# RWKV6 attention and an exact-GELU MLP in one kernel: the interleaving order of six of its eight stages rewritten

## The chip, the cores and the metric

The kernel runs on one core of a Trainium2 chip. A core has several engines that work side by side, each through its own queue in order: TensorE (PE in the profile, with its weight loads as a row of their own, PEld), VectorE (DVE), ScalarE (ACT), GpSimd (POOL) and SyncE (SP), which here only issues transfers. The metric is the time on the device in microseconds (us). Before the change the median of three runs is 587.15 us (586.81 to 588.11).

## The reference

Two blocks follow each other. The first is a recurrent attention over 4 batches, 8 heads, 768 tokens and 48 channels a head:

```python
for t in range(S):
    cur = np.einsum('bhd,bhe->bhde', u[None] * kt, vt)
    y[:, :, t] = np.einsum('bhd,bhde->bhe', rt, state + cur)
    state = wt[:, :, :, None] * state + np.einsum('bhd,bhe->bhde', kt, vt)
```

Its result, laid out as 3072 tokens by 384 channels, goes through an MLP with 2048 hidden channels:

```python
h = x @ w_in
g = 0.5 * h * (1.0 + erf(h * inv_sqrt2))
return g @ w_out
```

All data are float32.

## The kernel before, in words

**Passes and stages.** The 768 tokens of each batch are cut in two, so there are 8 pieces of 384 tokens. The outer loop (L1403) has a pass x for each, 0 to 7; "stage n" is the pass x = n. A stage runs the MLP of the piece before, `mlp(x-1)`, beside the attention of its own piece, `attention(x)`, and the beginning of the attention that follows, `attention(x+1)`. Behind stage 7, `mlp(7)` runs alone.

**Streams, pieces and the plan.** Each of these functions is a generator, and what it issues between two `yield`s is a piece. The order in which the engines get their instructions is written out by hand: `PLAN[x]` is a string, and each letter takes the next piece from one stream. `.` is `mlp(x-1)`; `s` the rest of `attention(x)`; `f` the beginning of `attention(x+1)`; `l` the loads of the next piece of r, w, k and v (`load`, L180); `x` the sums of this piece's MLP input that the next MLP wants (`sums_of_x`, L941; in stage 7 `sums_of_x15`, L984); `w` in stage 2 the sums of the weights (`first_sum`, `h_sums`, L895, L920) and in stage 7 those of `sums_of_w15` (L959); `c` converts weights in stages 0 and 1. A letter whose stream is at its end, or empty, does nothing. Behind the string the streams are emptied in the order `. s l x w`:

```python
        for c in PLAN[x]:
            next(streams[c], None)
        for c in ".slxw" if x == 0 else ".slxwc":
            while next(streams[c], streams) is not streams:
                pass
        slots = following
```

So a plan sets the order of the pieces in every engine's queue at once, and the order in which tiles are taken from the pools. Within a stream the order is fixed.

**The MLP** computes its products by schemes with fewer multiplications (7 block products where 8 would be needed), so that VectorE adds where TensorE would multiply.
- `h_halves` (L1028; MLPs 2 to 6) goes through four values of q. Each piece is one group of matmuls on 128x192 blocks (L1024), `first(q)` to `seventh(q)`; `first`, `fifth` and `sixth` are 2 matmuls, the others 4. `first` and `fifth` take a bank of the tag "mm", of which there are two; ScalarE copies results to the `u` banks or applies the Gelu (L1053, L1056, L1087, L1091), and `third` and `seventh` end in a VectorE addition (L1078, L1096). The order is first, third(q-1), seventh(q-1), second, fifth, sixth, fourth(q-1); `fourth(3)` is done late, inside the first product.
- The MLP of stage 2, `mlp(1)`, still goes through 16 whole h blocks (L1231 to L1246: 3 matmuls of 128x384 at L1236, then a Gelu at L1239).
- The second half is made of products (`product`, L1248): 8 matmuls at L1250, with a `yield` behind the fourth, so that a plan places half products. Each matmul has two records in the trace. Even MLPs have 7 products and 2 more that end in L1344 and L1347; odd MLPs have 7 and 5 more, and end in the addition L1373 after L1358, L1363, L1366 and L1369. `of_g` (L1010) makes the sums that the products need. The products also use the two "mm" banks, under the name `o_ps`.
- `h_fifteen` (L1140) is the form of `mlp(7)`.

**The attention** (`attention`, L366), from stage 2 on, is a chain of pieces:
1. VectorE multiplies out decays and products of r and k (L404 to L453; L404 is the first, and with L391 and `apart` it builds the sums within blocks of four tokens).
2. The layout for the first level: ScalarE's copies L573, VectorE's L578 and L579.
3. Bursts of 64x64 matmuls (L604), each into a pair of PSUM banks. There are two pairs from stage 2 on. The first level has three "fine" bursts of 20, 20 and 8 + 16 matmuls, the last with those of L595; the copies that empty them are VectorE's L637, and two "fine copies" at L687. At the second level odd pieces have three bursts of 20, 20 and 8 matmuls (the last 16 records in the trace, and it takes the pair of banks that the first leaves), even pieces one burst in three parts, the third part in the `u` banks. ScalarE's copies L620 empty these; a copy out of the `u` banks is twelve instructions, the others six.
4. Between them VectorE scales r and k (L658 to L669), and transposes blocks of k (L552); twelve moves of such blocks go through SyncE's queue (L547), eight from one piece and four from the next.
5. L749 multiplies the transposed k with v; it waits for those twelve moves. Then VectorE chains the states (L771, L773).
6. `inside()` (L802) multiplies within the chunks, into the pair `y_ps`; a ScalarE copy of the last result column, the *fence* (L815; in stage 0 VectorE's L812), stands behind it. The next piece (L845) adds the part of the states into the same banks; ScalarE copies the result to the MLP's input `xT` (L868), and through `ysb` (L871) and SyncE's transfers L875.

In each stage TensorE goes to and fro between the MLP's 128-wide matmuls and the attention's 64x64 ones; one stay with the second kind is called a visit below.

Of the kernel before, what the change touches and what calls it, by code (L numbers as in the profile page):

```python
# [41 lines left out]
        ".cswc.ccc.cccss.lc.ccscs..cc.cs.cclwcsc.ccssc.c.cccsccc..ssccc.c.lcls.cc.ccsc.w.clwscclccc"  # L42
        ".c.swcw.ss.ccs.lcsc..cwcccslccslff..w..fw.wfs..f..flffffffww"
    ),
    2: "...l...s..ws.swssswssss.sslsw...ssss.sssws.ll..ws.w..lw.sw.wl.sls.sls..lf.s....sf..f.f.xx.fxl.x.x",
    3: "l..sss..s.s..s.s....s...s.ssllss.sss.s.s.ss.l..lsss..sssss.sls.s..s......s..ls.llssf.sf.sflf.f.x.x..xxfffxf",
    4: "...s...lsl......s.s....sss..ssss..s..ss..s..s...llssslss....s.slss...s...sll.sl.s.sfs..fsf.ff..xl.x.xfffxffx",
    5: ".l..........ls.ss...s.sslls.ssss..ss.sls...sss..sssssl.ss.s..s.......s.lssll.sfsf.f.s.ff.x..x.xxxl",
    6: "sss.sls.....s......ls.s....s.sssssss..s.....s.ss....s.s.ssss.s.l.ss.l.ls.l...s.l.lslssf..s.ffs..lff.xx..xffxffx",
    7: "......s.s....s.s...s.ssssss...sss.ss...sss..ssss.s...ss.ww.ww.wwsw.ww.ww.ws.s.ss.s.ww.swww.swwwwwwww.wwww.www.xxxx.xxxxxx",  # L50
}


# [1436 lines left out]
```

## Time and profile before

| what | value |
| --- | --- |
| median of three runs | 587.15 us |
| the profiled execution's own time | 589.49 us |
| its span in the trace | 587.3 us |
| granted TensorE clock, mean | 0.997 |
| matmuls of the first half of the MLPs 2 to 6 with the two "mm" banks (L1024, `h_ps`) | 408, 81.4 us |
| matmuls of the h blocks (L1236) | 192, 64.1 us |
| first matmul of the MLP in stage 3, 4, 5, 6, 7 | 191.4, 255.7, 327.2, 391.4, 462.1 us |
| first matmul of `mlp(7)` | 526.8 us |
| HBM traffic, mean over the span | 70 GB/s |

The profile comes from one execution. Its lines give, for each engine, what ran when, and in brackets how long the engine had been idle before and what released it: `[0.31 <-PE d L604]` reads "idle for 0.31 us until TensorE's work at line 604 on the tile d was done". Start-to-start times of consecutive matmuls say what a matmul costs when TensorE is kept fed; the duration of one matmul record is longer, because matmuls overlap.

### The profile page before, as it was taken

To read this page: it belongs to the slowest core of one execution; us is meant where nothing else is said; L and a number is where in the kernel's file an instruction comes from. 1 tells how busy PE (TensorE), PEld (TensorE's weight loads), DVE (VectorE), ACT (ScalarE), POOL (GpSimd) and SP (SyncE) were. 2 spreads that over 40 slices of the span, in tenths; PEclk is the share of its full clock that TensorE was granted. 3 is DMA by queue.
4 is the path that set the end of the run, shared out by engine and by line. 5 is a ranking of instruction groups with operands and counts; after the bars stand their busy time and mean duration, and the time that the engine had idled before them with its cause. 6 is when DMAs were issued, how large, how long until landed. Compare 5 with 4: busy or idle time off the path is not lost. (4 is left out here: it accounts for less than half of the span.)

```text
span 587.3 us, 17363 instructions
## 1 busy us (share of the span) xinstructions
PE 572.2 (97%) x7505; PEld 508.6 (87%) x7517; DVE 460.5 (78%) x817; ACT 286.5 (49%) x668; POOL 8.0 (1%) x21
## 2 busy tenths in 40 slices
PE   7789999999999999999999999999999999999998
PEld 3576666766899999999999999999999999999997
DVE  6879766999969986787859987598768998975532
ACT  2468889322722558146462458245562465623400
POOL 3100000000000000000000000000000000000000
PEclk9989999999999999999999999999999999999999
DMA  7659661120142301341023310430015200210000
GB/s 241 207 159 356 217 213 56 36 87 2 31 139 79 110 2 32 97 126 38 1 39 106 124 39 18 97 104 19 2 28 168 73 3 1 41 40 8 1 15 33
DMA packets 51003, 46.79 MB, mean 80 GB/s; under 512 B 31728, under 2 KB 36080, under 8 KB 50928
## 3 DMA queue, kind: packets, MB, share of 16 engines
q1 hardware_dynamic: 50832, 45.62, 25.7%
q8 instruction: 59, 0.97, 0.7%
q14 instruction: 16, 0.13, 0.1%
q10 hardware_dynamic: 96, 0.07, 0.0%
HBM read 36.24 MB, written 4.72 MB: 70 GB/s over the span
## 5 line engine op out<-in xcount | busy, mean ns | idle before, releaser
L1024 PE MATMUL h_ps<-xT,w_in_sb 128*128 128x192 f32 x408 | 81.4, 330 | 1.0 <-DVE o_sb L1373 0.5
L1024 PEld LDWEIGHTS h_ps<-xT,w_in_sb 128*128 128x128 f32 x408 | 67.8, 190 | 4.1 <-ACT g L1056 1.2
L1236 PE MATMUL h_ps<-xT,w_in_sb 128*128 128x384 f32 x192 | 64.1, 490 | 0.1
L1236 PEld LDWEIGHTS h_ps<-xT,w_in_sb 128*128 128x128 f32 x192 | 35.9, 190 | 23.9
L1250 PE MATMUL o_ps<-w_out_sb,g 128*128 128x192 f32 x224 | 39.5, 326 | 0.0
L1250 PEld LDWEIGHTS o_ps<-w_out_sb,g 128*128 128x128 f32 x224 | 36.9, 190 | 0.3
L620 ACT COPY a_sb<-d 32x256 f32<-32x256 f32 (+8 forms) x90 | 32.6, 362 | 4.6 <-PE d L604 3.1
L1250 PE MATMUL o_ps<-w_out_sb,f 128*128 128x192 f32 x176 | 31.7, 330 | 0.0
L1250 PE MATMUL o_ps<-t,g 128*128 128x192 f32 x176 | 31.4, 329 | 0.0
L1250 PE MATMUL o_ps<-w_out_sb,e 128*128 128x192 f32 x176 | 31.3, 328 | 0.0
L1250 PE MATMUL o_ps<-t,s 128*128 128x192 f32 x176 | 30.9, 327 | 0.0
L1250 PE MATMUL o_ps<-t,e 128*128 128x192 f32 x176 | 30.9, 327 | 0.0
L1024 PE MATMUL u_ps<-s,w_in_sb 128*128 128x192 f32 x160 | 29.5, 327 | 0.0
L465 PEld LDWEIGHTS d<-rkw 64*64 64x64 f32 x1152 | 19.0, 134 | 11.9 <-issue 7.4
L637 DVE COPY_PREDICATED a_sb<-quarter,d 128x480 f32<-128x480 uint8 (+5 forms) x54 | 23.2, 438 | 7.7 <-PE d L604 6.4
L1250 PEld LDWEIGHTS o_ps<-t,g 128*128 128x128 f32 x176 | 28.7, 190 | 0.4
L1250 PEld LDWEIGHTS o_ps<-w_out_sb,e 128*128 128x128 f32 x176 | 28.8, 190 | 0.3
L1250 PEld LDWEIGHTS o_ps<-w_out_sb,f 128*128 128x128 f32 x176 | 28.7, 190 | 0.4
L1250 PEld LDWEIGHTS o_ps<-t,s 128*128 128x128 f32 x176 | 28.9, 190 | 0.1
L1250 PEld LDWEIGHTS o_ps<-t,e 128*128 128x128 f32 x176 | 28.8, 190 | 0.1
L604 PE MATMUL d<-kx,rkw 64*64 64x96 f32 x1056 | 28.2, 248 | 0.0
L604 PEld LDWEIGHTS d<-kx,rkw 64*64 64x64 f32 x1056 | 23.1, 133 | 5.8 <-issue 5.0
(240 smaller groups left out, 1178.8 us busy)
## 6 DMA issues: line engine op xcount, KB each, us to landing
rkw<-in_rkw_dram SPq DMA_DIRECT2D x54, 256.0 KB, 4.1
raw<-in_w_out_dram SPq DMA_DIRECT2D x8, 768.0 KB, 5.3
v_in<-in_v_dram SPq DMA_DIRECT2D x8, 584.0 KB, 4.0
raw<-in_w_in_dram SPq DMA_DIRECT2D x5, 768.0 KB, 8.5
out_dram<-o_sb SPq DMA_DIRECT2D x20, 192.0 KB, 1.9
rkw<-kx SPq DMA_DIRECT2D x72, 48.0 KB, 2.0
rkw<-in_rkw_dram SPq DMA_DIRECT2D x6, 384.0 KB, 6.1
raw<-in_w_in_dram SPq DMA_DIRECT2D x9, 256.0 KB, 4.6
```

The lines of the kernel that those rows point to most:

```text
L465: nc.tensor.matmul(d[half[p], g, n * width:(n + 1) * width], lhsT=kc[half[g], b, i, p], rhs=right(half[g], b, i, p), start=True, stop=True)
L604: nc.tensor.matmul(o[half[p], i * 3 * C // 2:(i + 1) * 3 * C // 2], lhsT=kc[half[g], n // NI, n % NI, p], rhs=rx[half[g], 2 * n + p], star ...
L620: nc.scalar.copy(out=at[z, g, first:behind, (a + 1) * h:], in_=d[z, :, :, to] if g == slice(None) else d[z, :, to])
L637: nc.vector.copy_predicated(out=an[:, :, :, :, (a + 1) * h:], mask=mask.to_broadcast(data.shape), data=data)
L1024: nc.tensor.matmul(o, lhsT=lhsT, rhs=rhs, start=start, stop=True, skip_group_check=True)
L1236: nc.tensor.matmul(h_ps, lhsT=w_in_sb[:, f // FI, j, f % FI * 128:(f % FI + 1) * 128], rhs=xT[:, j, :], start=(j == 0), stop=(j == NJ - 1))
L1250: nc.tensor.matmul(o, lhsT=lhs(j), rhs=rhs(j), start=start and j == 0, stop=(j == HF - 1), skip_group_check=True)
```

## The change

The strings of the stages 2 to 7 are replaced; stages 0 and 1, all functions and the number of pieces of each stream stay as they are. Each new string is six to eight letters longer than the old one, since it has letters that do nothing (a `c`, a `w` in stages 3 to 6, or one more call of a stream that is at its end). The number of working `f` letters is the same in each stage as before, so every attention is cut between two stages at the same piece. What differs is where the pieces stand against those of the other streams: which half product or which matmul group a burst, a load, a sum or a transposition stands behind.

```diff
-    2: "...l...s..ws.swssswssss.sslsw...ssss.sssws.ll..ws.w..lw.sw.wl.sls.sls..lf.s....sf..f.f.xx.fxl.x.x",
-    3: "l..sss..s.s..s.s....s...s.ssllss.sss.s.s.ss.l..lsss..sssss.sls.s..s......s..ls.llssf.sf.sflf.f.x.x..xxfffxf",
-    4: "...s...lsl......s.s....sss..ssss..s..ss..s..s...llssslss....s.slss...s...sll.sl.s.sfs..fsf.ff..xl.x.xfffxffx",
-    5: ".l..........ls.ss...s.sslls.ssss..ss.sls...sss..sssssl.ss.s..s.......s.lssll.sfsf.f.s.ff.x..x.xxxl",
-    6: "sss.sls.....s......ls.s....s.sssssss..s.....s.ss....s.s.ssss.s.l.ss.l.ls.l...s.l.lslssf..s.ffs..lff.xx..xffxffx",
-    7: "......s.s....s.s...s.ssssss...sss.ss...sss..ssss.s...ss.ww.ww.wwsw.ww.ww.ws.s.ss.s.ww.swww.swwwwwwww.wwww.www.xxxx.xxxxxx",
+    2: "..c....s.w.slsl.lssswss..sss.s.sss.slsssswwwwls.s.sl.w.....wwsllsl.s.s..slfssw.....f..fx.wxf.xxx..f....lx",
+    3: (
+        "..lcsssw.l..ss.ss....s....s.sss.ss.ss.ss.lllss...sss...sss.lss.....ss.s...s.sl..llsss.fssf"
+        ".ll.fxxfx.xx...ffsxfff."
+    ),
+    4: (
+        "s........css.....s..l..slss.ss..sss.....ssss...l.s.ssssll.l.sss..s...s....sllssls...f..ssf"
+        "f..ff..x..sxxlfxfwxxfflf"
+    ),
+    5: "......s......ss.ll..ss.sss.lsssssss....w..sss..slssss.ssl.sl...s.....sls.llss.fss.l...sc.xxxx.ff..xf.lfx",
+    6: (
+        "lsl..sl.........sssss...sl.....l..sssc.sss.sssss.....s.w.ssssl...sssss........sssss..l.lsl"
+        "lf.slff.s.ff..xx...xfxxxfff"
+    ),
+    7: (
+        "..s..s..s....s....sss..sss.ssssss......sss..swcwssswss...ssw.wswwl...wwww...sss.sww..wwwws"
+        "www..s.wwwswwwwwwwxwx.xxxxxw...xw.xxwx"
+    ),
```

## The prediction

> **What bounds the kernel now.** I read the page first, then the waits of TensorE, then the timelines around the places that the new plans touch. Stage n is the pass x = n of the outer loop, so the diff's third to eighth stage are stages 2 to 7.
>
> ```profile
> PE 572.2 (97%) x7505; PEld 508.6 (87%) x7517; DVE 460.5 (78%) x817; ACT 286.5 (49%) x668; POOL 8.0 (1%) x21
> ...
> PE   7789999999999999999999999999999999999998
> ```
>
> TensorE is busy in every slice behind the first three, so the end is set by TensorE's own sequence: a time changes only where that sequence gets a hole, loses one, or changes at its seams. In the trace a 128x192 matmul record follows the one before it 163 ns later, a pass of one product (8 matmuls, two records each) takes 2.6 us, and the stages add up from such records with little over. VectorE (78%) and ScalarE matter only where TensorE waits for them. This is who it waited for in stages 2 to 7, weight loads first in line:
>
> ```profile
> PEld h_ps L1024 <- DVE o_sb L1373: 1.2, 2, 0.8
> PEld h_ps L1024 <- DVE o_sb L1347: 1.0, 2, 0.6
> ...
> PEld kv_ps L749 <- DMA rkw<-kx: 0.2, 1, 0.2
> ```
>
> The first two rows are the seams between stages: the second matmul group of an MLP needs the PSUM bank that the last VectorE addition of the MLP before it reads (L1373, L1347). From the starts of the matmuls these seams cost 0.17, 0.59, 0.35, 0.31 and 0.80 us (stages 2/3 to 6/7); 0.17 is the floor, since VectorE was waiting for TensorE there. Smaller holes: L749 waits for the moved blocks of k in stages 3 and 4 (some 0.2 and 0.3 us), and the third burst of L604 waits 0.17 us for the copy of the first (L637) in stages 3, 5 and 7. Together 3.2 us: more can't be won from waits.
>
> **The change, part by part.** No instruction is added, so the sum has only seams and holes. Expanding both plans gives the order of pieces on each engine; I walked the new order with the durations of the old rows.
>
> *1. Seams between the two kinds of matmul.* A visit of 64x64 matmuls among 128x128 ones costs, in start-to-start times, 256 instead of 163 ns on entry, 148 instead of some 38 on leaving, and 267 instead of 163 behind it. The plans keep the number of visits except that in stages 2 to 5 the piece with L802 and the piece with L845 become neighbours (nothing of TensorE between them). That saves 0.148 + 0.104 + 0.093 = 0.345 us each. But L845 must wait for the fence, a ScalarE copy that reads the end of L802's result. The one place where they are neighbours now is stage 0:
>
> ```profile
> 39.24 1.53 PE L802 MATMUL y_ps<-a_sb,v_in 64*64 64x64 f32 x43
> ...
> 40.70 0.29 DVE L812 COPY fence<-y_ps 128x1 f32<-128x1 f32 x2 [0.89 <-PE y_ps L802]
> ...
> 41.04 1.41 PE L845 MATMUL y_ps<-rkw,st 64*64 64x64 f32 x38 [0.27 <-DVE fence L812]
> ```
>
> From the last L802 start to the first L845 start it is 0.577 us. In stage 2 ScalarE's fence ends 0.45 us behind the last L802, which agrees. Net +0.23 us, four times: **+0.9 us**. Bounds: -0.35 each if the fence were free, +0.3 each if L845's own second start (87 ns over) stays.
>
> The Trainium skill (TensorEngine Tiling (Array Packing), Key Properties) says that changing the tiling mode drains TensorE; the 256 and 267 ns agree. By that rule alone four merged visits would save four drains, 1.4 us; the 0.577 us row speaks against it, and the rule's case stands below as a rival.
>
> *2. Stage 2, first product of the second pair.* Now the Gelu of the last h block (155.33) stands ahead of the twelve copies of the third burst (155.72, L620):
>
> ```profile
> 151.85 2.26 ACT L620 COPY a_sb<-d 32x256 f32<-32x256 f32 x6
> 154.13 0.49 ACT L1239 ACTIVATE g<-h_ps 128x384 f32<-128x384 f32 x1
> 155.33 0.49 ACT L1239 ACTIVATE g<-h_ps 128x384 f32<-128x384 f32 x1 [0.71 <-PE h_ps L1236]
> 155.72 3.26 ACT L620 COPY a_sb<-u_ps 32x128 f32<-32x128 f32 x12
> ```
>
> The new plan puts the twelve copies ahead of it: 154.13 + 0.4 + 3.3 = 157.8, Gelu until 158.3. The product that takes that block's bank starts at 157.73 now: **+0.6 us** (0 to 0.7). L749 is then also one half product (1.3 us) earlier against moves that land at 164.0: **+0.15**.
>
> *3. Layout before the first burst, stage 7.* The burst (L604 at 478.13) needs the layout that VectorE ends with L579. VectorE works without a hole from the seam on:
>
> ```profile
> 463.03 0.35 DVE L1373 TENSOR_TENSOR o_sb<-o_ps,u 128x192 f32<-128x192 f32 x1
> ...
> 475.69 0.56 DVE L578 TENSOR_TENSOR kx<-rkw,tot_sb 128x384 f32<-128x384 f32 x1
> 476.65 0.96 DVE L579 TENSOR_TENSOR kx<-kx,tot_sb 128x768 f32<-128x768 f32 x1 [0.40 <-ACT kx L573]
> ```
>
> The layout ends 14.2 us behind the end of L1373, with 0.4 us to spare. The new plan has the same VectorE pieces in that stretch but the burst one group (second(2), 1.3 us) earlier: 14.05 us of VectorE against a burst that is 0.9 us too early: **+0.85** (0.4 to 1.1). In stage 3 the same move leaves 0.1 us, in 4 and 5 the lead shrinks to 0.3 to 0.5, in 6 it grows; no cost taken there.
>
> *4. The late burst of odd stages 5 and 7.* The addition of third(2) (L1078) now stands behind the fine copies (L687). In stage 5 it ends at 355.05, not 353.0, and in ScalarE's queue the Gelus of L1053 and L1056 wait for it, with the six copies of L620 behind them:
>
> ```profile
> 353.78 0.30 ACT L1053 ACTIVATE g<-g 128x128 f32<-128x128 f32 x1
> 353.98 0.41 ACT L1056 ACTIVATE rkw<-g 128x256 f32<-128x256 f32 x1
> 354.29 0.47 ACT L1087 COPY g<-h_ps 128x384 f32<-128x384 f32 x1
> 355.06 2.59 ACT L620 COPY a_sb<-d 32x320 f32<-32x320 f32 x6 [0.31 <-PE d L604]
> ```
>
> 355.05 + 0.2 + 0.3 + 0.4 brings the copies to 356.0 and their end to 358.65. The last burst takes the pair of banks that they free and starts at 358.06: +0.6 in stage 5, and by the same steps +0.5 in stage 7, **+1.1** (0 to 1.6). In stage 3 two more matmul groups lie between, and nothing is lost.
>
> *5. What goes.* The 0.17 us of the third burst in stages 3, 5 and 7 go, since a group now lies between (**-0.5**). Seams: in 3/4 the sums of x (L947) run before the last products, and VectorE reaches L1347 with 0.1 us to spare: -0.4. In 5/6 -0.15. In 4/5 the second sum now comes behind L1373 and takes its place: 0. In 6/7 VectorE is full from L404 (waiting for k's loads) to L1373, so only the earlier loads help: -0.35. Together **-0.9** (-1.4 if all reach the floor; +1 if a transfer of xT takes 3.8 us, as three did in stage 3, and not 1.9). L749: -0.2 in stage 4, +0.15 in 3 and 6: 0.
>
> Of the moved queue pieces, the twelve block moves keep their SyncE order behind the loads, and L749 stays behind the last landing in 5 and 7; the additions of weights moved forward in stage 7 delay the transposes by 1 us, and the landing still comes 0.6 us before L749.
>
> Sum: 0.9 + 0.6 + 0.15 + 0.85 + 1.1 - 0.5 - 0.9 = **+2.2 us**. The profiled execution took 589.49 us, with a span of 587.3 and 2.2 around it; the median of the runs, 587.15, is 0.4% below it. So 589.5 for the span, 591.7 for that execution, and 587.15 + 2.2 = **589.3 us** for the median.
>
> **Rivals.** What a measurement of this kernel can tell is about 0.2%, 1.2 us either way.
> - *The holes don't open* (16%): ScalarE and VectorE reach points 2, 3 and 4 in time, since each misses by under 1 us in a queue walked by hand. Then 587.15 + 0.9 - 0.5 - 0.9 = 586.7: no change. For it: TensorE's own delays upstream give VectorE time. Against: VectorE shows no hole in the 14 us of point 3.
> - *VectorE leads at each seam* (13%, the other side): if L1373 and L1347 always come within 0.2 us behind the last matmul, the five seams lose 1.4 us, the bursts 0.5 and L749 0.5, and with the merged visits at their 0.345 us saved and not lost, the kernel wins 3.8 us: 583.4; with the fence paid as in stage 0, 585.7. The point from which it decides: VectorE's backlog at the last product, under 0.2 us in all five. For it: the sums of x stand earlier in all stages. Against: the 6/7 chain from L404 on.
> - *The merged visits save* (4%): L845 follows L802 with no wait, because the fence's copy is over in time; then four times 0.345 us go and 0.9 are not lost: 587.15 + 2.2 - 0.9 - 1.4 = 587.05, no change. Against: the 0.577 us row. This is what the Trainium skill's drain rule (section above) gives by itself.
> - *Lateness adds up* (10%): L749 comes 1.3 us earlier in stages 2, 5 and 7; if the moves land late by the 1.2 to 1.8 us that single issues of them show, or xT by 1.9, some 3 us more: 592.
> - The forecast (57%): 588 to 591.
>
> The range takes in the lateness as far as 592.0 and the seams as far as 586.0. The forecast lies within 0.2% with 5 of its 57: faster 13%, same 25%, slower 62%.
>
> **What would show it.** L802 and L845 neighbours with some 0.58 us between their last and first start in stages 2 to 5 (point 1); ScalarE's Gelu of the last h block near 158 us, and a hole ahead of o_ps (2); L604 waiting for L579 in stage 7 (3); L604 waiting for L620 before the 16-record burst in 5 and 7 (4); seams of 0.17 to 0.35 us but for 6/7 (5). I am wrong if L845 follows without its wait, or if VectorE's pieces before the first burst take less than in the old order.

## The result, and the profile after

The new plans make the kernel slower: 592.37 us (median of six runs, 589.92 to 592.97) against 588.25 us for the kernel before in six runs (586.81 to 589.21). The ratio is 1.0056 with a 95% interval of 1.0036 to 1.0077, or +3.3 us (2.1 to 4.5; the two medians themselves lie 4.1 us apart); forecast were +2.2 us. The profiled execution took 592.04 us with a span of 590.0.

In the kernel after, all lines behind the plans stand 12 further down: L802 is L814, L845 is L857, L1347 is L1359. The page's first row first:

```profile
PE 571.1 (97%) x7505; PEld 507.8 (86%) x7517; DVE 459.4 (78%) x817; ACT 285.6 (48%) x668; POOL 8.0 (1%) x21
```

The work is the same to 0.3% on every engine. The time came in as waits of TensorE. This is the view of the waits (who waited for whom: us in all, times, longest):

```profile
PEld d L616 <- ACT a_sb L632: 1.7, 2, 0.9
PEld h_ps L1036 <- DVE o_sb L1359: 1.4, 2, 1.2
...
PEld y_ps L857 <- ACT fence L827: 1.2, 4, 0.3
...
PEld o_ps L1262 <- ACT g L1251: 0.7, 1, 0.7
...
PEld h_ps L1036 <- DVE o_sb L1385: 0.4, 1, 0.4
```

The first, third and fourth row are new (L604 for L620, L845 for the fence, a product for the h block's Gelu). Of the two seam rows of before, L1347's has grown from 1.0 to 1.4 us and L1373's has shrunk from 1.2 to 0.4.

Stage by stage, from the first 128-wide matmul of one stage to that of the next (us):

| kernel | start of 2 | 2 | 3 | 4 | 5 | 6 | 7 | 2 to 7 |
| --- | --- | --- | --- | --- | --- | --- | --- | --- |
| before | 118.67 | 72.68 | 64.21 | 71.60 | 64.05 | 70.88 | 64.50 | 407.92 |
| after | 118.34 | 73.91 | 64.09 | 72.39 | 64.63 | 70.95 | 64.91 | 410.88 |

So +2.96 us in the six stages; stages 0 and 1, which are unchanged, were 0.33 shorter in this execution, and `mlp(7)` took 57.83 us from its first matmul to the end of its last in both. (Counted so, the stages before begin at 255.56, 391.21 and 526.59 us, where the table ahead of the prediction has 255.7, 391.4 and 526.8, about one matmul record later.) From the start-to-start times, each place of the prediction gets a measured value (a visit is counted from the last matmul before it to the second one behind it, less those matmuls' own 163 or 323 ns):

| step | forecast | measured |
| --- | --- | --- |
| 1 merged visits L802/L845, stages 2 to 5 | +0.9 | +0.60 (0.154, 0.146, 0.153, 0.147) |
| 2 stage 2: Gelu behind twelve copies; L749 | +0.6; +0.15 | +0.72; +0.35 |
| 3 stage 7: first burst waits for the layout | +0.85 | +0.28 |
| 4 last burst in 5 and 7 | +1.1 | +1.29 (0.64, 0.65) |
| 5 third burst's wait gone, stages 3, 5, 7 | -0.5 | -0.46 (-0.22, -0.02, -0.22) |
| 5 seams 3/4, 4/5, 5/6, 6/7 | -0.4, 0, -0.15, -0.35 | **+0.56**, -0.02, -0.15, -0.45 |
| 5 L749 in 3, 4, 6 | 0 | +0.11, +0.07, +0.21 |
| not forecast: second burst of the second level, 3, 5, 7 | | -0.48 |
| not forecast: product of stage 7 behind twelve copies | | +0.32 |

The rows add up to 2.95. Each is the difference of two single executions; the terms that depend on transfers (the seams and L749) scatter most, as the runs below show.

The merged visit of stage 2, all engines:

```profile
172.18 0.28 PE L857 MATMUL y_ps<-rkw,st 64*64 64x64 f32 x2
...
172.42 0.16 ACT L827 COPY fence<-y_ps 128x2 f32<-128x2 f32 x1 [0.55 <-PE y_ps L814]
172.63 0.30 PEld L857 LDWEIGHTS y_ps<-rkw,st 64*64 64x64 f32 x12 [0.31 <-ACT fence L827]
```

The last L814 starts at 172.13, so L857 gets going 0.50 us later, 0.05 behind the end of the fence; two records of it go ahead of the wait. Stage 2's h blocks, ScalarE:

```profile
153.80 0.49 ACT L1251 ACTIVATE g<-h_ps 128x384 f32<-128x384 f32 x1
154.19 3.26 ACT L632 COPY a_sb<-u_ps 32x128 f32<-32x128 f32 x12
157.48 0.49 ACT L1251 ACTIVATE g<-h_ps 128x384 f32<-128x384 f32 x1
```

The twelve copies have gone ahead of the last Gelu, which now ends at 158.0 (forecast: 158.3). Stage 5, ScalarE and then TensorE:

```profile
356.53 0.31 ACT L1065 ACTIVATE g<-g 128x128 f32<-128x128 f32 x1 [1.12 <-DVE g L1090]
...
357.41 2.59 ACT L632 COPY a_sb<-d 32x320 f32<-32x320 f32 x6
```

```profile
360.05 0.56 PE L616 MATMUL d<-kx,rkw 64*64 64x96 f32 x16 [0.56 <-ACT a_sb L632]
```

The Gelu waits 1.12 us for the addition behind the fine copies, the six copies follow it, and the last burst waits for them. Stage 7, TensorE, the first burst, which now waits for the end of the layout (L579 is L591):

```profile
478.87 1.88 PE L616 MATMUL d<-kx,rkw 64*64 64x96 f32 x80 [0.21 <-DVE kx L591]
```

The seam of stages 3 and 4, VectorE, before and then after:

```profile
251.35 0.35 DVE L1319 TENSOR_TENSOR o_sb<-o_ps,u 128x192 f32<-128x192 f32 x1
251.62 2.19 DVE L398 TENSOR_TENSOR kx<-rkw,rkw 128x1152 f32<-128x1152 f32 x1
255.63 0.36 DVE L947 TENSOR_TENSOR s<-xT 128x192 f32<-128x192 f32 x1 [1.82 <-DMA xT<-ysb]
256.02 0.36 DVE L947 TENSOR_TENSOR xT<-xT 128x192 f32<-128x192 f32 x1
256.30 0.35 DVE L1347 TENSOR_TENSOR o_sb<-o_ps,rkw 128x192 f32<-128x192 f32 x1
```

```profile
252.60 0.56 DVE L436 TENSOR_TENSOR tot_sb<-tot_sb 128x384 f32<-128x384 f32 x1
255.06 0.36 DVE L959 TENSOR_TENSOR s<-xT 128x192 f32<-128x192 f32 x1 [1.90 <-DMA xT<-ysb]
...
255.73 1.11 DVE L436 TENSOR_TENSOR tot_sb<-tot_sb 128x192 f32<-128x192 f32 x4
...
257.69 0.35 DVE L1359 TENSOR_TENSOR o_sb<-o_ps,rkw 128x192 f32<-128x192 f32 x1
```

After the change VectorE stands idle for 1.9 us in front of the first sum of x, because the fifth and the sixth transfer of xT landed 3.3 and 2.9 us after their issue and not 1.9. Behind this sum queue a second one, 1.1 us of L436 (L424 of before) that could have been done meanwhile, three more sums, and only then the addition that the next stage's second group waits for: it starts 2.63 us behind the start of the first sum. Before, VectorE waited 1.8 us at the same place, for three late transfers, but had done its L424 by then, and the addition stood behind two sums: 0.67 us.

### The profile page after: what moved, and what is told of

Same layout as the page of the kernel before. It is cut to its first block, busy times and chain, and to the rows that moved or that the text cites. A ratio compares the mean times of both kernels' runs of the same rounds, so it can differ in the third digit from the quotient of the medians.

```text
span 590.0 us, 17365 instructions
## 1 busy us (share of the span) xinstructions
PE 571.1 (97%) x7505; PEld 507.8 (86%) x7517; DVE 459.4 (78%) x817; ACT 285.6 (48%) x668; POOL 8.0 (1%) x21
## 5 line engine op out<-in xcount | busy, mean ns | idle before, releaser
L616 PE MATMUL d<-kx,rkw 64*64 64x96 f32 x1056 | 26.8, 246 | 1.3 <-ACT a_sb L632 1.1
L1251 ACT ACTIVATE g<-h_ps 128x256 f32<-128x256 f32 (+1 forms) x32 | 13.9, 433 | 29.2 <-PE h_ps L1248 28.6
```

The source lines that it names most:

```text
L616: nc.tensor.matmul(o[half[p], i * 3 * C // 2:(i + 1) * 3 * C // 2], lhsT=kc[half[g], n // NI, n % NI, p], rhs=rx[half[g], 2 * n + p], star ...
L1251: nc.scalar.activation(out=gs[group][:, f % FG, 0:t], in_=h_ps[:, 0:t], func=AF.Gelu)
```

## Experiments

Times of single executions scatter by 3 us and more, in good part because stages 0 and 1 end anywhere between 117.0 and 120.6 us in these traces, whatever the later plans say. The lengths of stages, by contrast, repeat to 0.05 us where nothing near them was changed and no transfer fell differently (stage 6: 70.94 to 70.97 in eight of the nine traces that have its new plan unchanged, 70.88 or 70.89 in the three with the old). So the experiments are read by stages, against the table above; all but the last two are single executions. "New plans" and "old plans" are those of the kernels after and before.

### visits_split

```diff
-    5: "......s......ss.ll..ss.sss.lsssssss....w..sss..slssss.ssl.sl...s.....sls.llss.fss.l...sc.xxxx.ff..xf.lfx",
+    5: "......s......ss.ll..ss.sss.lsssssss....w..sss..slssss.ssl.sl...s.....sls.llsss.fs.l...sc.xxxx.ff..xf.lfx",
...
```

(the same step in 2, 3 and 4)

> The new plans, but in stages 2 to 5 the piece with L802 stands one half product earlier, so that it and L845 are two visits again. In the traces a merged visit is 0.15 us longer than the two single visits of the old plans (3.43 against 1.75 + 1.52, 3.66 against 1.75 + 1.755). Theory A (the wait for the fence costs more than the saved change of matmul kind): visits of 1.75 and 1.52 or 1.755 us, each of the stages 2 to 5 shorter by 0.15 us, 0.6 in all. By the prediction's own term it would be 0.23 each, 0.9 in all. Rival (the Trainium skill, TensorEngine Tiling (Array Packing), Key Properties: a change of tiling drains TensorE): four more drains, 0.345 us each, stages longer by 1.4 us in all.

Two visits of 1.755 and 1.521 or 1.755 us in all four stages, as in the old plans. Stage 2: 73.74 (-0.17), 3: 63.97 (-0.12), 5: 64.48 (-0.15). Theory A holds, and the rival, longer stages by four drains, is excluded. Stage 4 came out at 71.32 (-1.07), far more: in this execution all six transfers of xT landed in 1.9 us, the hole of the seam fell from 1.10 to 0.43 us, and L749 waited 0.23 us less. The 0.43 us that are left are no transfer's: with L802 earlier, VectorE waited 1.68 us for the product that the addition L1319 reads, with L416 queued behind it, and then ran without a wait to the seam.

### addition_first

```diff
-    5: "......s......ss.ll..ss.sss.lsssssss....w..sss..slssss.ssl.sl...s.....sls.llss.fss.l...sc.xxxx.ff..xf.lfx",
+    5: "......s......ss.ll..ss.sss.lsssss...ss.w..sss..slssss.ssl.sl...s.....sls.llss.fss.l...sc.xxxx.ff..xf.lfx",
...
-        "..s..s..s....s....sss..sss.ssssss......sss..swcwssswss...ssw.wswwl...wwww...sss.sww..wwwws"
+        "..s..s..s....s....sss..sss.ssss...ss...sss..swcwssswss...ssw.wswwl...wwww...sss.sww..wwwws"
```

> The new plans, but in stages 5 and 7 the group third(2) with its addition stands ahead of the two fine copies again. Theory A (the Gelu behind this addition holds up ScalarE's copies, and these the last burst): the last burst's visit falls from 1.33 and 1.34 us to 0.69, the visit of the two bursts before it rises from 2.01 to 2.17, since the second burst then waits for the fine copies; stages 5 and 7 shorter by 0.48 us each. Rival (VectorE and ScalarE have a backlog in these stages, and a hole that is closed opens at the next burst): the last burst still waits over 0.4 us, the stages change by less than 0.2 us.

Last burst 0.69 us in both stages, the two bursts before it 2.17 and 2.18; stage 5: 64.17 (-0.46), stage 7: 64.46 (-0.45). Theory A, to 0.03 us. The hole did not open elsewhere.

### totals_before_sums

```diff
-        ".ll.fxxfx.xx...ffsxfff."
+        ".ll.ffxxx.xx...ffsxfff."
```

> The new plans, but at the end of stage 3 VectorE's products L424 (the five behind the first) stand ahead of the sums of x instead of among them. Theory A (1.1 us of L424 and the sums queue behind a sum that waits 1.9 us for a transfer, and L1347 behind all of them): VectorE does L424 while it waits, L1347 starts 1.1 us earlier, the hole in the second matmul group of stage 4 falls from 1.10 to some 0.15 us, 0.95 us gained. Rival (the transfers of xT, three of which take 3 to 3.3 us, set the seam by themselves): the sums still start when the last transfer has landed, and the hole shrinks by less than 0.3 us.

Stage 4: 71.58 (-0.81). The fifth and sixth transfer were late again (3.7 and 3.3 us), and VectorE did the five L436 first:

```profile
251.93 1.71 DVE L436 TENSOR_TENSOR tot_sb<-tot_sb 128x384 f32<-128x384 f32 x5
254.79 0.36 DVE L959 TENSOR_TENSOR s<-xT 128x192 f32<-128x192 f32 x1 [1.16 <-DMA xT<-ysb]
...
256.52 0.35 DVE L1359 TENSOR_TENSOR o_sb<-o_ps,rkw 128x192 f32<-128x192 f32 x1
```

The hole is 0.60 us, where addition_first, with the same landing (1.06 us ahead of the stage's first matmul) and the sums among L436, has 1.49: 0.89 us by the order alone. The remaining 0.6 us are put down to the late transfer; no run shows this order with all transfers in time and L802 beside L845. Both theories have a part, and the order has the larger one in this pair of runs.

### copies_and_moves

```diff
-    2: "..c....s.w.slsl.lssswss..sss.s.sss.slsssswwwwls.s.sl.w.....wwsllsl.s.s..slfssw.....f..fx.wxf.xxx..f....lx",
+    2: "..c....s.w.slsl.lssswss..sss.s.sss.slsssswwwwls..ssl.w.....ww.sllsls.s..slfssw.....f..fx.wxf.xxx..f....lx",
...
```

(and one half product or group moved in 3, 4 and 6)

> The new plans with five places put right that the trace shows as holes. Stage 2: the twelve copies L620 stand behind the last h block's Gelu again; L749 stands one half product later in stages 2, 4 and 6; in stage 3 the last scaling of k and its transposes stand one matmul group earlier. Theory A (each hole is the lateness at its own place, and nothing else moves): hole of 0.62 us in stage 2 gone, L749's visits fall to 1.74 us from 2.10, 2.20, 2.25 and 1.95; stages 2, 3, 4, 6 shorter by 0.97, 0.46, 0.50 and 0.20 us, 2.1 in all. Rival (the chain behind L749 is the bound, and a later L749 only moves the wait): L845 begins to wait for the states (its lead over the end of the chain is 2.1, 3.5 and 2.5 us now) and gives back more than half.

Stage 2: 74.11 (+0.20). The hole at the Gelu is gone, but another of 1.18 us opened one product later: the four copies L745 (L733 of before) now stood behind the twelve and ahead of the copy that frees the product's bank. Stages 4 and 6: L749 no longer waits (1.74 us), but VectorE's chain of states starts later against the matmuls, and at the seams 4/5 and 6/7 holes of 0.46 + 0.76 and 0.59 + 0.89 us stand where 0.23 and 0.25 stood; stages 5 and 7 became 0.63 and 0.80 us longer, stage 6 0.39. This is what the rival says, with the difference that the wait reappears at the seam and not at L845. Stage 4 is 1.08 us shorter all the same, since its seam with stage 3 had no hole this time: of the six transfers of xT only the last was late (3.2 us). Stage 3: the moves landed 1.1 us earlier and L749's visit stayed at 2.20 us, so it was not waiting for them. ScalarE of the kernel after shows for what:

```profile
232.75 4.23 ACT L632 COPY a_sb<-d 32x320 f32<-32x320 f32 x12
237.01 0.32 ACT L1307 COPY o_sb<-o_ps 128x192 f32<-128x192 f32 x1
237.22 2.08 ACT L745 COPY rkw<-kx 32x384 f32<-32x384 f32 x4
```

L749 gets going at 239.36, with the end of L745; the last move had landed at 239.21.

### three_stages

```diff
-    2: "..c....s.w.slsl.lssswss..sss.s.sss.slsssswwwwls.s.sl.w.....wwsllsl.s.s..slfssw.....f..fx.wxf.xxx..f....lx",
+    2: "..c....s.w.slsl.lssswss..sss.s.sss.slsssswwwwls..sl.w....s.wwsllsl.s.s..slfssw.....f..fx.wxf.xxx..f....lx",
...
-        "..lcsssw.l..ss.ss....s....s.sss.ss.ss.ss.lllss...sss...sss.lss.....ss.s...s.sl..llsss.fssf"
+        "..lcsssw.l..ss.ss....s....s.sss.ss.ss.ss.lllss...sss...sssss.ssl.s......s...sl..llsss.fssf"
...
-        "..s..s..s....s....sss..sss.ssssss......sss..swcwssswss...ssw.wswwl...wwww...sss.sww..wwwws"
+        "..s..s..s....s.....sss..sssssssss......sss..swcwssswss...w.swwwl..s.wwww.s..sss.sww..wwwws"
```

> The new plans with the order of stages 2, 3 and 7 changed at the places of their holes. Stage 2: the twelve copies L620 behind the last h block's Gelu, and this time also the four copies L733 five half products later, so that they do not stand ahead of the copy L1286. Stage 3: transposes ahead of seventh(3), the copies L620 and L733 two to five pieces earlier. Stage 7: the first burst one group later, the third burst one group later, the twelve copies L620 behind the last Gelus of the MLP. Theory A (each hole comes from one piece that stands ahead of another in one engine's queue; all of the queue between has to be read, not just the pair): stage 2 loses its hole of 0.62 us, stage 3 the 0.46 us that L749 waits (for ScalarE's L733, not for the moves), stage 7 0.28 us before the first burst and 0.22 us at the product: 73.3, 63.6 and 64.4 us. Rival (VectorE and ScalarE are full in these stages; a hole that is closed opens elsewhere): stages 2 and 7 shorten by less than 0.25 us, and new holes stand in the list.

Stage 2: 73.22 (-0.69) and no hole; stage 3: 63.64 (-0.45), L749's visit 1.74 us. Theory A for both. Stage 7: 66.11 (**+1.20**), the rival's case: with the first burst a group later, its wait is gone, but TensorE now reaches that group's bank too early, and ScalarE has it behind the layout:

```profile
476.71 1.34 ACT L585 COPY kx<-rkw 128x384 f32<-128x384 f32 x3 [1.09 <-DVE rkw L444]
...
478.84 0.48 ACT L1079 COPY u_ps<-h_ps 128x384 f32<-128x384 f32 x1
```

L585 (L573 of before) waits for VectorE, L1079 queues behind it, and a group waits 0.95 us for L1079; the second and the last burst of the second level are late by 0.5 and 0.8 us (the last by 0.65 in the new plans). VectorE has no slack in the first 14 us of stage 7; the burst's 0.28 us were only the first place at which that showed. The product's hole of 0.32 us is gone.

### old_two_costs

```diff
-    5: ".l..........ls.ss...s.sslls.ssss..ss.sls...sss..sssssl.ss.s..s.......s.lssll.sfsf.f.s.ff.x..x.xxxl",
+    5: ".l..........ls.ss...s.sslls.ssss..ssss.l...sss..sssssl.ss.s..s.......s.lssll.sfsf.f.s.ff.x..x.xxxl",
...
```

(the same in 7; in 2, 3 and 4 the `s` with L802 moved behind the halves of products that stood between it and L845)

> The old plans with two of the new plans' orders put in: in stages 5 and 7 the two fine copies stand ahead of third(2) and its addition; in stages 2, 3 and 4 L802 stands right ahead of L845. Theory A (these orders cost by themselves, whatever else the plan does): stages 5 and 7 longer by 0.48 us each (the last burst 0.64 later, the second burst's wait of 0.16 gone), stages 2, 3 and 4 by 0.15 us each: 72.83, 64.36, 71.75, 64.53 and 64.98 us. Rival for the merged visits (the drain rule of the Trainium skill, TensorEngine Tiling (Array Packing), Key Properties, without a wait): 0.345 us shorter each. Rival for stages 5 and 7 (the cost needs the new plans' density around it): under 0.2 us.

The last burst's visit rose to 1.33 and 1.34 us, the pair before it fell to 2.01: +0.48 and +0.49 at these places, and stages 5 and 7 became 0.37 and 0.40 us longer, since their seams were shorter by 0.11 and 0.08 in this execution. The merged visits are 3.43, 3.66 and 3.43 us: +0.15 each, as in the new plans. Stage 2 got a further hole of 0.25 us at a product, stages 3 and 4 were shorter by 0.22 and 0.70 us, because L749 and the seam did not wait this time (no late transfer). Theory A; "they save a drain" and "under 0.2 us" are out.

### loads_late

```diff
-        "lsl..sl.........sssss...sl.....l..sssc.sss.sssss.....s.w.ssssl...sssss........sssss..l.lsl"
+        "ls..s.........sssss.l..s.......sssc.sss.sssss.....s.w.ssss...sssss.l..l.l.l...sssss.l.ll.s"
```

> The new plans with the loads of stage 6 issued where the old plan issued them. Theory A (VectorE is full from L404 to L1373, and L404 waits for the loads of k; the earlier loads are what shortened the seam of stages 6 and 7): VectorE waits some 0.4 us for a load ahead of L404 again and the hole at the second matmul group of stage 7 grows from 0.25 to some 0.65 us; stage 7 0.4 us longer. Rival (the order of VectorE's own pieces shortened the seam): hole stays at 0.25 us, within 0.1.

```profile
453.32 3.08 DVE L416 SCALAR_TENSOR_TENSOR kx<-rkw,u_sb 128x384 f32<-128x384 f32 x4 [1.64 <-DMA rkw<-in_rkw_dram]
```

VectorE waits 1.64 us for the load ahead of L416 (L404 of before), and the seam 6/7 has holes of 0.87 + 0.89 us where 0.25 stood; stages 6 and 7 are 0.89 and 0.76 us longer. The direction is theory A's, the size four times what it said: issued in a row, the loads landed 6 us after their issue, against 4.9 us with the old plan and 3.2 to 4.1 with the new. So late loads do lengthen this seam; that they alone made the difference between the old plan and the new is not shown by it.

### old_tail_of_3, new_tail_in_old, v_load_later

The seam 3/4 is where the prediction failed; three runs are about it.

```diff
-        "..lcsssw.l..ss.ss....s....s.sss.ss.ss.ss.lllss...sss...sss.lss.....ss.s...s.sl..llsss.fssf"
-        ".ll.fxxfx.xx...ffsxfff."
+        "..lcsssw.l..ss.ss....s....s.sss.ss.ss.ss.lllss...sss...sss.lss.....ss.s...s.sl.s.llssf.sf."
+        "sflf.f.x.x..xxfffxf"
```

> The new plans, with the end of stage 3 (from the product of L1307 on) in the old order. In the five traces of the new order in which the fifth transfer of xT landed 3.3 to 3.9 us after its issue the second matmul group of stage 4 waited 1.1 to 1.7 us for L1347 (0.6 with L424 ahead of the sums). Theory A (the order in VectorE's queue decides what a late transfer costs): with the old order the hole is 0.5 us or less with late transfers and 0.1 to 0.2 without, as in the two traces of the old order; stages 3 and 4 together shorter by 0.75 us or more (0.15 of it from L802 and L845 apart). Rival (the transfers by themselves): a late fifth or sixth transfer brings a hole of over 0.9 us here too.

No transfer was late, and no hole but the usual 0.1 us stood at the seam; stage 4 71.16 (-1.23). Behind the new start of stage 3 the old end opened a hole of 0.19 us at a product, so stage 3 was no shorter (64.16). Inconclusive between the two theories, since the late transfer did not occur.

```diff
-    3: "l..sss..s.s..s.s....s...s.ssllss.sss.s.s.ss.l..lsss..sssss.sls.s..s......s..ls.llssf.sf.sflf.f.x.x..xxfffxf",
+    3: "l..sss..s.s..s.s....s...s.ssllss.sss.s.s.ss.l..lsss..sssss.sls.s..s......s..l.llsss.fssf.ll.fxxfx.xx...ffsxfff.",
```

> The old plans, with the end of stage 3 (from the product of L1307 on) in the new order. Theory A (this order by itself lets a late transfer cost more): where the fifth transfer of xT lands 3.3 us or more after its issue, the hole at the second group of stage 4 is 1.1 us or more, against 0.49 with the old order and three late transfers; stage 4 longer by 0.6 us, stage 3 by 0.15 for the merged visit. Where no transfer is late the hole is under 0.45 us. Rival (the hole needs the new plan's earlier parts of stage 3): 0.5 us or less although the fifth transfer is late.

The fifth and sixth transfer landed after 3.9 and 3.4 us, and the hole is 1.63 us; stage 4 72.31 (+0.71, with L749's wait absent). The old order had 0.49 us although its fifth transfer landed later still, 0.1 us ahead of the stage's first matmul (here 0.9 ahead). So theory A: the order costs it, without the rest of the new plan.

```diff
-        ".ll.fxxfx.xx...ffsxfff."
+        "..fxxfx.xx...llffsxfff."
```

> The new plans, with the load of v in stage 3 issued behind the last product and not right behind the six transfers of xT. In the traces SyncE's queue pauses by 0.3 to 1.3 us at about the 74th, 107th, 121st, 140th, 175th and 208th of its 244 transfers, and the one to three transfers issued just before land in 2.3 to 3.9 us and not in 1.9; the load of v is the 121st. Theory A (the place in the count decides, not the load): the fifth or the sixth transfer of xT still lands after 2.8 us or more, and the hole at the second group of stage 4 stays over 0.9 us. Rival (the 0.6 MB of v, issued right behind, hold up the small transfers): all six land in 1.9 us, and the hole falls under 0.45 us.

The fifth and sixth transfer again took 3.8 and 3.4 us, the pause fell on the store that is now the 121st transfer (counting from 0), and the hole was 1.60 us. The load of v is not the cause. That the place in the count is the cause is not shown: the store was issued right behind the six transfers, where the load had stood.

### mixed, mixed_again

Both put together what the runs so far had shown (plans of 2, in the second also of 4, as before; the others as after with the moves named).

> Stage 2 as in the old plans; stages 3 to 7 as in the new ones with the orders changed that earlier runs or the list of holes showed to cost: L802 and L845 apart in 3 to 5, the products L424 ahead of the sums of x and the copies L620 and L733 earlier in 3, third(2) ahead of the fine copies in 5 and 7, the third burst one group later in 5, the twelve copies behind the last Gelus in 7; stage 6 unchanged. Theory A (the losses are separate places and their sum): stages of 72.7, 63.5, 71.2, 63.8, 70.95 and 64.2 us, 406.4 in all, against 407.9 with the old plans and 410.9 with the new: 0.26% faster than the kernel before. Rival (holes that are closed open elsewhere, as in stage 7 of the run before): over 408 us, no faster than before.

Ratio to the kernel before 1.0005 (0.9988 to 1.0022): no difference. The stages are 72.68, 63.49, 71.80, 64.46, 70.97 and 64.17 us, 407.57 in all: of the 4.5 us that the list of holes promised against the new plans, 3.3 came. The rest went into two places that the moves themselves opened: 0.8 us at the seam 3/4, though no transfer was late (L802 ahead of a half product made VectorE wait 1.64 us for that product's addition L1319, with L416 behind it), and 0.8 us in stage 5, where the third burst, a group later, held up the second level.

> Stages 2 and 4 as in the old plans; stage 3 as in the new plan up to its last products, with the copies L620 and L733 and the transposes earlier, and with the old plan's end; stages 5 and 7 as in the new plans with third(2) ahead of the fine copies, in 5 with L802 and L845 apart, in 7 with the twelve copies behind the last Gelus; stage 6 as in the new plan. Theory A (sum of separate places): 72.7, 63.5, 71.1, 64.0, 70.95 and 64.2 us, 406.4 in all against 407.9 with the old plans: 0.25% faster than the kernel before. Rival (what one place gives, the next takes): 407.5 us or more, no difference from the kernel before.

Ratio 1.0014 (0.9994 to 1.0033), stages 72.68, 63.78, 71.38, 64.33, 71.20 and 64.13, 407.50 in all. The seam 3/4 is at its floor, but the old end of stage 3 behind its new start opened the hole at a product again (0.29 us); L749 waited 0.64 and 0.46 us in stages 4 and 6 this time, and L802 0.31 us in stage 5. No version was measured to be faster than the kernel before.

## Why the prediction was right, and where it was not

- **Direction and size** were right: a sum of small holes on TensorE, none of it work. +2.2 us was forecast, 2.96 us are in the stages, +3.3 us (2.1 to 4.5) in the runs. In absolute terms the median of 592.37 us lies above the forecast's 588 to 591 and 0.4 us above the end of the range; the kernel before, run along, was itself 1.1 us above the median that the forecast started from, and 587.15 us times the measured ratio is 590.4. That the sum came so close is in part luck: row by row the forecast was too low by 2.2 us in all and too high by 1.5, and these cancel.
- **1, merged visits**: right in sign, 0.15 and not 0.23 us each. The row taken was stage 0's (0.577 us), which has two VectorE fence copies, the second starting 0.13 us behind the first; the others have one ScalarE copy, and 0.50 us. That the merge costs is shown from both sides (visits_split, old_two_costs). By the drain rule of the Trainium skill (TensorEngine Tiling (Array Packing), Key Properties) alone it should have saved the rows' 0.345 us each; the trace agrees with the drains (256 and 267 ns) and differs in the sum, because 0.50 us from the last L802 to the next L845 take their place.
- **2, the Gelu behind twelve copies**: right, 0.62 us and 0.10 for the second record behind the hole (three_stages takes it away). L749 was sized 0.2 us too small.
- **3, the burst of stage 7**: right in mechanism, 0.28 and not 0.85 us. VectorE took 13.6 us from the end of L1373 to that of L579 and not 14.05 (14.2 before): the wait for ScalarE's L573 fell from 0.40 to 0.1 us, and the same instructions between follow each other by 0.36 us closer in their new order. So the sign of being wrong that the prediction named, VectorE taking less than in the old order, came true in part. three_stages shows that to move the burst a group later doesn't win the time back: TensorE then waits 0.95 us at the next place.
- **4, the late burst of 5 and 7**: right, 1.29 against 1.1 us, shown both ways (addition_first, old_two_costs). The same order frees a pair of banks earlier for the second burst, -0.16 us in each odd stage, which the prediction did not see. Its list of holes was short by this: counted by visits, the kernel before held 0.16 us at the second burst of stages 3, 5 and 7, and 0.35 and 0.43 us (not 0.2 and 0.3) at L749 in stages 3 and 4.
- **5, the third burst**: the sum was right (-0.46 for -0.5), the steps were not. The wait was 0.22 us and not 0.17 in each of the three stages; it went in 3 and 7, but in stage 5 it stayed, since the first two bursts stand together there and the copy of the first (L637, L649 of after) ends at 347.01 us, 0.15 ahead of the third burst. The group between, two matmuls, is too short.
- **5, the seams**: three of four right. The step that failed is "in 3/4 the sums of x (L947) run before the last products, and VectorE reaches L1347 with 0.1 us to spare: -0.4". It came out at +0.56. The condition beside it, "+1 if a transfer of xT takes 3.8 us", was in essence met in six of the seven executions with the merged L802 and L845 in front of this tail and the sums among L424: the fifth transfer took 3.3 to 3.9 us, and the hole was 1.1 to 1.7 us, so against the 0.49 us of before the usual price is nearer +1 than the +0.56 of this execution. The error was to price the late transfer as bad luck of before, since its trace had three (3.8, 3.3 and 2.9 us), and to walk the queue with landings of 1.9 us. Whether the new order also brings the lateness on is open: all eight executions with the new end of stage 3, or a variant of it, and the merged visits had a late transfer of xT in stage 3, of the six others only that of the kernel before. In 6/7 loads_late fits the prediction's reason; the hole at the second group was 0.70, 0.62 and 0.43 us in the three executions with the old plan of stage 6 and 0.23 to 0.32 with the new.
- **L749** in 3: the prediction put it down to the moves; in the new order it was ScalarE's L733 (copies_and_moves, three_stages). In 2, 4 and 6 it does wait for the last move: it gets going within 0.15 us of that landing.
- **Rivals**: "the holes don't open", "VectorE leads at each seam" and "the merged visits save" are out; "lateness adds up" had a part in it, at the seam 3/4.

## What to carry to other kernels

When an order of pieces changes and no work does, list TensorE's start-to-start excess place by place and walk the queue of each engine that feeds it; a hole is set by one instruction that stands behind another. Most such terms were forecast to 0.3 us here; two missed by 0.6 and 1.0 us, because VectorE's instructions followed each other closer than walked and because transfers came late. Do not let an instruction that waits for a transfer stand ahead of work that could run meanwhile: that is where 0.9 of the 1.5 us of the worst hole came from in the pair of runs that compares the orders (addition_first, totals_before_sums). And holes do not simply add up when they are closed: in the run `mixed` three quarters of the sum came back, and the rest reopened in two places that the moves themselves had opened.

## What the runs showed of the hardware

- SyncE's transfers have pauses at much the same places of their count. In nearly every trace one transfer near each of the 72nd, 107th, 141st, 175th and 209th of 244 (within four to six places) takes 0.9 to 1.9 us to issue where its neighbours take 0.3 to 0.7, and most of the one to three before it land after 2.3 to 3.9 us, not 1.9; in some traces more fall near the 113th, 121st, 146th and 212th. Moving a load from the 121st place left the pause there, at what came 121st (v_load_later; all places counted from 0). Whether the count, the moment or the kind of the transfers in front decides was not separated: in five of the fourteen traces no pause falls between the 115th and the 125th.
- The Trainium skill (DMA: Bandwidth & Descriptors, Anatomy of one DMA) gives a fixed cost of about 2.0 us per transfer, for another issuing path. The 1.82 to 1.92 us of most transfers of xT are close to that; the pauses are not in it. What makes them was not found.
- The time to the start of stage 2 differed by 3.6 us between executions of identical early code (117.0 to 120.6 us). The longest came with a mean granted clock of 0.994 over the execution, the shortest with 1.0. A plan's difference of 1 us is readable in stage lengths long before it is in the time of a run.
